# The last 96 rows of an MLP's output weights, moved to 24 lanes and to another DMA queue

## Chip, cores and metric

The kernel runs on one core of a Trainium2 chip. The metric is the device time of one execution in microseconds (us); the median of several timed runs counts, and lower is better. A profiled execution, taken separately, gives the trace. Engines: PE multiplies matrices, DVE (VectorE) works element by element, ACT (ScalarE) evaluates functions and copies, POOL (GpSimd) makes constants, SP (SyncE) only issues DMAs. ACT can issue DMAs too, in a queue of its own. A "lane" is one of the 128 partitions of the on-chip memory.

## What is computed

One decoding step of a transformer block: attention over a cache and a gated MLP, both on the same normalised input, added to that input. The input has 4 rows of 640 numbers; attention has 32 heads of 128 with a cache of 4096 positions; the MLP has 2 x 864 hidden units. All inputs are bf16.

```python
def _A_ref(x, k_cache, v_cache, wq, wo):
    q = (x @ wq).reshape(B, Sq, Hq, Dh).transpose(0, 2, 1, 3)
    scores = jnp.einsum('bhqd,bhkd->bhqk', q, k_cache) * Dh ** (-0.5)
    o = jnp.einsum('bhqk,bhkd->bhqd', _softmax(scores), v_cache)
    return o.transpose(0, 2, 1, 3).reshape(B, Sq, Hq * Dh) @ wo

def _B_ref(x, w_in, w_sp, b_sp, w_out):
    z = _gelu(jnp.einsum('bsd,df->bsf', x, w_in))
    z1, z2 = z[..., :Fh], _layernorm(z[..., Fh:])
    g = jnp.einsum('ts,bsf->btf', w_sp, z2) + b_sp[None, :, None]
    return jnp.einsum('bsf,fd->bsd', z1 * g, w_out)

xn = _layernorm(x)
return x + _A_ref(xn, ...) + _B_ref(xn, ...)
```

The two caches are 268 of the 282 MB that are read; everything else is small beside them.

## The kernel before

**Attention.** The work is cut into 16 units, one for each group of eight heads and batch row. A unit reads 8.4 MB of K and as much of V. Lane p holds 256 consecutive positions of one head. A unit's K comes in four runs of 64 positions a lane, into a ring of seven run buffers (`k_ring`); its V goes into one large buffer, `v_all`, of 64 KB a lane. For each run DVE multiplies K by the query (`product`, L493) and folds the halves (`fold_half`, L499), PE sums the folded products in eight steps (`sums`, L508), DVE finishes the row sums (`row_sums`, L521). Once a unit has its four runs come the maximum, the exponentials on ACT (L543), the spread by heads into `p_m` (L554) and the weighted sum over V on PE (`weighted`, L578), one unit later.

**Order.** The order on PE, DVE, ACT and SP is written by hand: the loop over n counts K runs, four for each unit. Loads stand in one list, `loads`, and are issued in that order on SP's queue by `pump()` as soon as the buffers they need are marked free. An issued load still waits, on SP, for the instructions that last used its buffer, and every load behind it on SP waits with it. DMA semaphores are dealt out in a circle of eight.

**The MLP.** Its weights have no buffer of their own. `w_q` and `w_in` lie in `v_all` before the first V load comes; the first 768 rows of `w_out` lie in `p_m` (six rows a lane, `w_out_sb`), and the last 96 rows, one a lane in lanes 0 to 95, lie in `v_all` behind `w_in` (`w_end_sb`, L101). `load_w` (L109 to L114) issues these three loads on SP between the two halves of the first unit's K. So SP's list begins: w_q, half of K of unit 0, w_in, w_out, the 96 rows, the other half of K of unit 0, K of unit 1, V of unit 0. V of unit 0 overwrites `w_in` and the 96 rows, and waits for the MLP's last products.

The generator `gmlp` (L351) does the MLP in pieces between the first K runs; `next(mlp)` runs it to its next `yield`. In order: the products with `w_in` (L361), 70 of them, with hidden units on the lanes of `zT`: for each half of the hidden units six groups of 128 lanes and, in the seventh column, one of 96; the copy to `zz` and GELU on DVE with a Tanh on ACT (L369 to L383); the sums for the layer norm (L388); its few scalars; the gate (L441 to L453); and the 14 products with `w_out` (L457), of which the last two use the 96 rows. They add into `out_ps`, where attention's projection (L639) adds later too. Piece one runs behind the sums of K run 0, two and three around the fold of run 1 and so on; the L457 products come after the fold of run 2 and before its sums, so on PE these sums stand behind them.

`NFC`, the number of groups of hidden units in each half (7), sets the width of all the tiles in between: `zz`, `gw`, `gt` have 2 x NFC x 4 = 56 columns, `gz` has three times 28, `yT` has 28.

Of the kernel before, what the change touches and what calls it, by code (L numbers as in the profile page):

```python
# [17 lines left out]
def kernel(  # L18
# [14 lines left out]
    nc = tc.nc  # L33
    P = nc.NUM_PARTITIONS
    Bsz, Sq, D = A_x.shape
    _, H, S, Dh = A_k_cache.shape
    HD = A_wq.shape[1]
    F = B_w_in.shape[1]
    Fh = F // 2
    DC = D // P  # L40
# [19 lines left out]
    QW = HC * Dh  # L60
    RING = 2 * NK - 1
    NFF = Fh // P
    NFC = NFF + 1
    FT = Fh - NFF * P
    NOH = D // 2
    CB = 4
    NG = NR // CB
# [25 lines left out]
    v_all = places.tile([P, NK * QW], BF16, name="v_all")  # L93
# [3 lines left out]
    w_in_sb = v_all[:, DC * HD : DC * (HD + F)].rearrange("p (c n) -> p c n", c=DC)  # L97
    w_out_sb = p_m[:].rearrange("p n g c h -> p (n g c h)")[:, 0 : NFF * D].rearrange(
        "p (k n) -> p k n", k=NFF
    )  # L100
    w_end_sb = v_all[:, DC * (HD + F) : DC * (HD + F) + D]  # L101
    nc.sync.dma_start(out=wq_sb, in_=A_wq.rearrange("(p c) n -> p c n", c=DC))

    wsp_bf = const.tile([1, 1], BF16)
# [4 lines left out]
    def load_w():  # L109
        nc.sync.dma_start(out=w_in_sb, in_=B_w_in.rearrange("(p c) n -> p c n", c=DC))  # L110
        nc.sync.dma_start(
            out=w_out_sb, in_=B_w_out[0 : NFF * P].rearrange("(p k) n -> p k n", k=NFF)
        )
        nc.sync.dma_start(out=w_end_sb[:FT], in_=B_w_out[NFF * P : Fh])  # L114

    def run_of(cache, u):
        hg, b = divmod(u, Bsz)
# [101 lines left out]
    for e in range(PAR):  # L219
        nc.gpsimd.tensor_copy(  # L220
            out=of_row[:, e, :, :, e, :],
            in_=ident[:].rearrange("p (k q) -> p q k", q=QD)[:, 0:Bsz, :, None].to_broadcast(
                [P, Bsz, NQ, LN]
            ),
# [15 lines left out]
    for i in range(NSTAT):  # L240
# [5 lines left out]
        out=rstd[:], in_=mv[:, 1:2], func=ACT.Sqrt, bias=eps_tile[:Bsz], scale=1.0  # L246
# [4 lines left out]
        out=xn_bf[:],  # L251
# [9 lines left out]
    for c in range(DC):  # L261
        nc.tensor.transpose(
            out=xnT_ps[:, c, :], in_=xn_v[:, c, :], identity=ident[:Bsz, :Bsz]
# [8 lines left out]
    for e in range(PAR):  # L272
        q_ps = ps_pv.tile([P, HG, Dh], FP32, tag="pv", name="q_ps")
        for c in range(DC):
            for k in range(NQ):
                nc.tensor.matmul(  # L276
                    out=q_ps[k * QD : (k + 1) * QD],
                    lhsT=xnT[:, c, :],
                    rhs=wq_v[:, c, k, e],
# [3 lines left out]
        rows = const.tile([P, HG, Dh], BF16, name=f"q_rows{e}")  # L283
        nc.vector.tensor_scalar(  # L284
            out=rows[:], in0=q_ps[:], scalar1=scale_qk, scalar2=None, op0=ALU.mult
# [7 lines left out]
        out=hot[:].rearrange("p c h -> p (c h)"),  # L293
        in_=ident[:].rearrange("p (g m) -> p m g", m=QD),
# [6 lines left out]
        out=pick[:, :, Bsz - 1 :].rearrange("p c (k q) -> p c k q", q=QD)[  # L301
            :, :, :, 0 : PAR * Bsz : Bsz
        ],
        in_=hot[:].rearrange("p c (e k) -> p c k e", e=PAR),
# [3 lines left out]
    with nc.allow_low_precision("0 and 1"):  # L308
        nc.vector.tensor_reduce(
            out=own[:],  # L310
            in_=ident[:].rearrange("p (h l) -> p h l", h=HT),
# [5 lines left out]
        out=par[:], in_=own[:].rearrange("p (k e) -> p e k", e=PAR), axis=AX.X, op=ALU.add  # L317
# [3 lines left out]
        out=far[:],  # L321
# [13 lines left out]
    for half in range(2):  # L335
        nc.tensor.matmul(
            out=out_ps[OG * half : OG * half + OG, :],
            lhsT=ident[:Bsz, :OG],
            rhs=x_bf[:, half * NOH : (half + 1) * NOH],
# [13 lines left out]
    def gmlp():  # L353
        zz, gw, gt, gz = (gm[n] for n in ("zz", "gw", "gt", "gz"))
        zT = ps_pv.tile([P, 2, NFC, Bsz], FP32, tag="pv", name="zT")
        for t in range(2):
            f1 = t * Fh + NFF * P
            w_t = w_in_sb[:, :, t * Fh : f1].rearrange("p c (f k) -> p c k f", k=NFF)
            for k in range(NFC):
                for c in range(DC):  # L360
                    nc.tensor.matmul(  # L361
                        out=zT[: P if k < NFF else FT, t, k, :],
                        lhsT=w_t[:, c, k, :] if k < NFF else w_in_sb[:, c, f1 : f1 + FT],
                        rhs=xnT[:, c, 0:Bsz],
                        start=(c == 0),
                        stop=(c == DC - 1),
                    )
        yield
        nc.vector.tensor_copy(out=zz[:, :, 0:NFF, :], in_=zT[:, :, 0:NFF, :])  # L369
        nc.vector.tensor_copy(out=zz[:FT, :, NFF, :], in_=zT[:FT, :, NFF, :])  # L370
        nc.vector.tensor_tensor(out=gw[:], in0=zz[:], in1=zz[:], op=ALU.mult)
        nc.vector.tensor_scalar(
            out=gw[:], in0=gw[:], scalar1=0.044715, scalar2=1.0, op0=ALU.mult, op1=ALU.add
        )
        nc.vector.tensor_tensor(out=gw[:], in0=gw[:], in1=zz[:], op=ALU.mult)
        nc.scalar.activation(
            out=gt[:], in_=gw[:], func=ACT.Tanh, scale=math.sqrt(2.0 / math.pi)
        )
        yield
        nc.vector.tensor_scalar(  # L380
            out=gt[:], in0=gt[:], scalar1=1.0, scalar2=0.5, op0=ALU.add, op1=ALU.mult
        )
        nc.vector.tensor_tensor(out=gz[:, 0:2], in0=zz[:], in1=gt[:], op=ALU.mult)  # L383
        sq = gz[:, 2, :, :]
        nc.vector.tensor_tensor(out=sq, in0=gz[:, 1, :, :], in1=gz[:, 1, :, :], op=ALU.mult)

        s_ps = ps_m.tile([1, 2, NFC, Bsz], FP32, tag="m", name="ln_ps")
        nc.tensor.matmul(  # L388
            out=s_ps[:], lhsT=ones_sq[:, 0:1], rhs=gz[:, 1:3], start=True, stop=True
        )  # L390
        yield
        st, ac = gm["st"], gm["ac"]
        mean_t = st[:, 0:Bsz]
        ex2_t = st[:, Bsz : 2 * Bsz]
        var_t = st[:, 2 * Bsz : 3 * Bsz]
        rst_t = st[:, 3 * Bsz : 4 * Bsz]
        tmp_t = st[:, 4 * Bsz : 5 * Bsz]
        nc.vector.tensor_reduce(
            out=st[:, 0 : 2 * Bsz].rearrange("o (s b) -> o s b", s=2),
            in_=s_ps[:].rearrange("o s k b -> o s b k"),  # L400
            axis=AX.X,
            op=ALU.add,
        )
        nc.vector.tensor_scalar(
            out=st[:, 0 : 2 * Bsz],
            in0=st[:, 0 : 2 * Bsz],
            scalar1=1.0 / float(Fh),
            scalar2=None,
            op0=ALU.mult,
        )  # L410
        nc.vector.tensor_tensor(out=tmp_t, in0=mean_t, in1=mean_t, op=ALU.mult)
        nc.vector.tensor_tensor(out=var_t, in0=ex2_t, in1=tmp_t, op=ALU.subtract)
        nc.scalar.activation(
            out=rst_t, in_=var_t, func=ACT.Sqrt, bias=eps_tile[:1], scale=1.0
        )
        wsp_t = work.tile([1, 1], FP32, name="wsp_t")
        nc.vector.tensor_copy(out=wsp_t[:], in_=wsp_bf[:])
        bsp_t = work.tile([1, 1], FP32, name="bsp_t")
        nc.vector.tensor_copy(out=bsp_t[:], in_=bsp_bf[:])
        yield  # L420
        nc.vector.reciprocal(out=rst_t, in_=rst_t)
        nc.vector.tensor_scalar(
            out=ac[:, 0:Bsz], in0=rst_t, scalar1=wsp_t[:, 0:1], scalar2=None, op0=ALU.mult
        )
        nc.vector.tensor_tensor(out=tmp_t, in0=ac[:, 0:Bsz], in1=mean_t, op=ALU.mult)
        nc.vector.tensor_scalar(
            out=ac[:, Bsz : 2 * Bsz],
            in0=tmp_t,
            scalar1=-1.0,
            scalar2=bsp_t[:, 0:1],  # L430
            op0=ALU.mult,
            op1=ALU.add,
        )
        ac_ps = ps_m.tile([P, 2 * Bsz], FP32, tag="m", name="ac_ps")
        nc.tensor.matmul(
            out=ac_ps[:], lhsT=ones_sq[0:1, :], rhs=ac[:], start=True, stop=True
        )
        ac_sb = work.tile([P, 2 * Bsz], FP32, name="ac_sb")
        nc.scalar.copy(out=ac_sb[:], in_=ac_ps[:])
        yield  # L440
        nc.vector.tensor_tensor(  # L441
            out=sq,
            in0=gz[:, 1, :, :],
            in1=ac_sb[:, None, 0:Bsz].to_broadcast([P, NFC, Bsz]),
            op=ALU.mult,
        )
        nc.vector.tensor_tensor(
            out=sq,
            in0=sq,
            in1=ac_sb[:, None, Bsz : 2 * Bsz].to_broadcast([P, NFC, Bsz]),  # L450
            op=ALU.add,
        )
        nc.vector.tensor_tensor(out=gm["yT"][:], in0=gz[:, 0, :, :], in1=sq, op=ALU.mult)  # L453
        for k in range(NFC):
            w = P if k < NFF else FT
            for half in range(2):
                nc.tensor.matmul(  # L457
                    out=out_sum(half),
                    lhsT=gm["yT"][:w, k, :],
                    rhs=(w_out_sb[:, k] if k < NFF else w_end_sb[:FT])[  # L460
                        :, half * NOH : (half + 1) * NOH
                    ],
                    start=False,
                    stop=False,
                )
        yield
# [206 lines left out]
    with tc.manual_schedule(engines={E.PE, E.DVE, E.Activation, E.SP}):  # L673
# [3 lines left out]
        for n in range(NK * NU):  # L677
# [55 lines left out]
            out=den[:],  # L733
# [62 lines left out]
```

## Time and profile before

| | us |
|---|---|
| timed runs, median of 3 (lowest to highest) | 662.78 (662.63 to 662.92) |
| the profiled execution | 667.55 |
| its span, from the first instruction to the last | 665.7 |
| DVE busy in the span | 522.6 (79%) |
| PE busy (matmul) | 307.7 (46%) |
| ACT busy | 29.7 (4%) |
| read from HBM | 282.24 MB, 424 GB/s over the span |

How to read it: "busy" is the time in which at least one instruction of the engine ran. The page cuts the span into 40 slices of 16.6 us and gives, for each, the busy share of every engine in tenths and what the core's 16 DMA engines moved. The table of queues gives packets, megabytes and the time their packets took, as a share of what 16 engines have. A packet is one contiguous piece that one DMA engine moves; a load of 128 lanes is 128 packets, eight for each engine, and at its end each engine adds one to the load's semaphore, by a packet of 4 bytes. The trace holds each packet with its start, duration and size, and each increment of a semaphore; where the text speaks of packet records or increments, it is these.

In lines of the timeline the first two numbers are the start and the duration in us, then come engine, line and operation, what is written and read, the shape, and how many such instructions are merged (x70); in brackets the engine's idle time before and what ended it. SPq and ACTq are the instructions that issue DMAs.

### The profile page before, as it was taken

What the parts mean: (1) busy time and instruction counts of PE and PEld (TensorE: products, weight loads), DVE (VectorE), ACT (ScalarE), POOL (GpSimd) and SP (SyncE); (2) the same over time, 40 slices, a digit from 0 to 9 for tenths busy, and PEclk for the clock granted to TensorE, in tenths of its full rate; (3) what the DMA queues carried; (4) which work ended last, traced back from release to release, by engine and by line L of the source; (5) the groups of instructions that cost most, each with busy time, mean ns of one, the idle gap of its engine ahead of it and who ended that gap; (6) DMA issues with size and microseconds to landing.
All of it is one profiled execution on the core that took longest, in us unless ns stands there. A gap on an engine that the chain in (4) does not pass through costs nothing.

```text
span 665.7 us, 4619 instructions
## 1 busy us (share of the span) xinstructions
PE 307.7 (46%) x1999; PEld 135.3 (20%) x1999; DVE 522.6 (79%) x326; ACT 29.7 (4%) x73; POOL 2.6 (0%) x12
## 2 busy tenths in 40 slices
PE   0264253624625364263536437263362634637357
PEld 0131021211302222122212212121120221213124
DVE  2576995969699594987959598595978969999950
ACT  0020000000000000000000000000000000000000
POOL 1000000000000000000000000000000000000000
PEclk9667586775767677586666867678585767866685
DMA  9999999999999999999999999999999999999996
GB/s 376 420 409 382 414 407 441 441 430 441 430 441 441 417 434 429 438 433 441 430 434 430 420 439 438 437 433 430 437 434 437 425 433 434 416 440 428 459 399 277
DMA packets 8417, 282.54 MB, mean 424 GB/s; under 512 B 865, under 2 KB 2125, under 8 KB 3277
## 3 DMA queue, kind: packets, MB, share of 16 engines
q1 hardware_dynamic: 8376, 282.24, 99.1%
q8 instruction: 15, 0.25, 0.1%
q14 instruction: 6, 0.04, 0.0%
q10 hardware_dynamic: 20, 0.01, 0.0%
HBM read 282.24 MB, written 0.01 MB: 424 GB/s over the span
## 4 chain that ended last, share of the span: by engine, by line
DMA 64%; DVE 26%; PE 8%; issue 1%; SPq 0%; DVEq 0%; ACT 0%
DMA k_ring<-in_A_k_cache_dram 57%; DVE k_ring L493 14%; DVE k_ring L499 7%; PE s_ps L508 7%; DMA v_all<-in_A_v_cache_dram 4%; DMA k_ring<-in_A_wo_dram 3%; DVE s_sb L521 2%; DVE p_m L554 1%; DVE m L530 1%; PE out_ps L639 1%; PE pv L578 1%; DVE mt L532 0%; DVE mt L535 0%; DVE nm L537 0%; DVE o_n L621 0%
## 5 line engine op out<-in xcount | busy, mean ns | idle before, releaser
L493 DVE TENSOR_TENSOR k_ring<-k_ring,qbc 128x8192 bf16<-128x8192 bf16 x64 | 282.7, 4418 | 96.8 <-DMA k_ring<-in_A_k_cache_dram 96.8
L508 PE MATMUL s_ps<-k_ring,ident 128*128 128x512 bf16 x512 | 197.8, 556 | 323.0 <-DVE k_ring L499 322.9
L508 PEld LDWEIGHTS <-ident 128*128 128x128 bf16 x512 | 64.7, 128 | 434.7 <-issue 381.5
L499 DVE TENSOR_TENSOR k_ring<-k_ring 128x4096 bf16<-128x4096 bf16 x64 | 146.0, 2281 | 0.0
L578 PE MATMUL pv<-v_all,p_m 128*32 128x512 bf16 x960 | 60.7, 410 | 0.0
L521 DVE TENSOR_REDUCE s_sb<-s_ps 128x64 f32<-128x512 f32 x64 | 43.7, 683 | 3.3 <-PE s_ps L508 3.3
L554 DVE TENSOR_TENSOR p_m<-p_c,own 128x2048 bf16<-128x2048 bf16 x16 | 36.6, 2285 | 0.7 <-ACT p_c L543 0.7
L578 PEld LDWEIGHTS <-p_m 128*32 128x32 bf16 x992 | 26.2, 104 | 41.5 <-issue 16.2
L543 ACT ACTIVATE p_c<-s_sb,nm 128x256 bf16<-128x256 f32 x16 | 8.1, 508 | 336.1 <-DVE nm L537 336.1
L609 PEld LDWEIGHTS o_ps<-o_rows,pick 128*128 128x128 f32 x96 | 20.7, 297 | 4.2 <-issue 3.2
L609 PE MATMUL o_ps<-o_rows,pick 128*128 128x128 f32 x96 | 19.6, 374 | 0.0
L590 ACT COPY o_rows<-pv 128x512 f32<-128x512 f32 x16 | 9.4, 585 | 168.8 <-PE pv L578 168.7
L284 DVE TENSOR_SCALAR q_rows<-q_ps 128x512 bf16<-128x512 f32 x2 | 1.4, 692 | 13.6 <-PE q_ps L276 13.6
L755 DVE TENSOR_TENSOR o_n_last<-o_last,rden_all 128x32 bf16<-128x32 f32 x1 | 0.2, 191 | 13.7 <-PE o_last L747 13.7
L483 ACT CAST qbc<-qbc_ps 128x128 bf16<-128x128 f32 x16 | 4.2, 265 | 105.2 <-PE qbc_ps L475 105.2
L276 PE MATMUL q_ps<-v_all,xnT 128*32 128x512 bf16 x40 | 3.8, 559 | 10.9 <-DMA v_all<-in_A_wq_dram 10.9
L530 DVE TENSOR_REDUCE m<-s_sb 128x1 f32<-128x256 f32 x16 | 6.7, 420 | 0.6
L475 PE MATMUL qbc_ps<-q_rows,of_row 128*128 128x128 bf16 x32 | 6.2, 284 | 0.6 <-DVE q_rows L284 0.6
L475 PEld LDWEIGHTS <-of_row 128*128 128x128 bf16 x32 | 4.3, 136 | 8.1 <-issue 7.6
L656 PE MATMUL o_last<-hot,o_rows 128*128 128x8 f32 x32 | 4.9, 279 | 0.7 <-ACT o_rows L590 0.7
L656 PEld LDWEIGHTS o_last<-hot,o_rows 128*128 128x128 f32 x32 | 4.8, 226 | 1.8 <-ACT o_rows L590 1.7
L578 PE MATMUL pv<-k_ring,p_m 128*32 128x512 bf16 x32 | 3.6, 631 | 2.8 <-DMA k_ring<-in_A_v_cache_dram 2.8
(88 smaller groups left out, 70.7 us busy)
## 6 DMA issues: line engine op xcount, KB each, us to landing
k_ring<-in_A_k_cache_dram SPq DMA_DIRECT2D x6, 4096.0 KB, 19.1
v_all<-in_A_v_cache_dram SPq DMA_DIRECT2D x2, 4096.0 KB
v_all<-in_A_wq_dram SPq DMA_DIRECT2D x1, 5120.0 KB
k_ring<-in_A_v_cache_dram SPq DMA_DIRECT2D x1, 4096.0 KB, 35.8
k_ring<-in_A_wo_dram SPq DMA_DIRECT2D x3, 1280.0 KB, 20.0
v_all<-in_B_w_in_dram SPq DMA_DIRECT2D x1, 2160.0 KB, 29.2
k_ring<-in_A_v_cache_dram SPq DMA_DIRECT2D x1, 2048.0 KB, 40.3
k_ring<-in_A_v_cache_dram SPq DMA_DIRECT2D x1, 1024.0 KB, 41.3
```

The lines of the kernel that those rows point to most:

```text
L475: nc.tensor.matmul(out=qb_ps[:], lhsT=of_row[:, e, b].rearrange("p k f l -> p (k f l)"), rhs=q_rows[e][:, hg, :], start=(e == 0), stop=(e ...
L493: nc.vector.tensor_tensor(out=t, in0=t, in1=qbcs[u][:, None, :].to_broadcast([P, HC, Dh]), op=ALU.mult)
L499: nc.vector.tensor_tensor(out=t[:, :, 0:HD2], in0=t[:, :, 0:HD2], in1=t[:, :, HD2:Dh], op=ALU.add)
L508: nc.tensor.matmul(out=s[:], lhsT=ident[:], rhs=t[:, :, g * RW : (g + 1) * RW], start=(g == 0), stop=(g == m - 1),)
L521: nc.vector.tensor_reduce(out=scores[u][:, r * HC : (r + 1) * HC], in_=sums_ps.pop(n)[:], axis=AX.X, op=ALU.add,)
L530: nc.vector.tensor_reduce(out=m1[:], in_=scores[u][:], axis=AX.X, op=ALU.max)
L543: nc.scalar.activation(out=p_c[u][:], in_=scores.pop(u)[:], func=ACT.Exp, bias=maxes.pop(u)[:], scale=1.0, accum_out=row_den[hg % NACC][:, ...
L554: nc.vector.tensor_tensor(out=p_m[:, u % 2], in0=p_c.pop(u)[:].rearrange("p (g c) -> p g c", c=CB)[:, :, :, None].to_broadcast([P, NG, CB, HT]
L578: nc.tensor.matmul(out=pvs[u][cg * QD : (cg + 1) * QD, :], lhsT=p_m[:, u % 2, g0 + n].rearrange("p c h -> p (c h)"), rhs=v_at[:, n * CB : ...
L590: nc.scalar.copy(out=o[:].rearrange("p c d -> p (c d)"), in_=pvs.pop(u)[:])
L609: nc.tensor.matmul(out=gr[hg][:], lhsT=pick[:, c, Bsz - 1 - b : P + Bsz - 1 - b], rhs=o[:, c, :], start=(b == 0 and c == 0), stop=(b == Bs ...
L656: nc.tensor.matmul(out=o_last[0][:, :, :, u % Bsz], lhsT=o[:, c, :], rhs=hot[:, c, :].rearrange("p (e k) -> p k e", e=PAR), start=(c == 0) ...
```

## The change

The 96 rows are laid out anew: row 4p + r of them goes to lane p, as the r-th of four in that lane, so they fill lanes 0 to 23 with 5,120 contiguous bytes each. The place in `v_all` is rounded up to a multiple of 256 elements. The load leaves SP's list; it is issued on ACT's queue instead, as four transfers, of which transfer l takes lanes l, l + 4, ..., l + 20. They stand in program order behind the products with `w_in` and so, on ACT, behind the second cast of a query (L483) and ahead of the table load for the Tanh (L376). The hidden units follow the rows: the last 96 of each half are taken in four groups of 24, every fourth unit, so NFC grows from 7 to 10, the products at L361 from 70 to 100 and those at L457 from 14 to 20, and the element-wise tiles from 56 to 80 and from 28 to 40 columns.

```diff
-    NFC = NFF + 1
-    FT = Fh - NFF * P
+    FR = 4
+    FT = (Fh - NFF * P) // FR
+    NFC = NFF + FR
+    LS = 4
...
-    w_end_sb = v_all[:, DC * (HD + F) : DC * (HD + F) + D]
+    end_at = -(-DC * (HD + F) // 256) * 256
+    w_end_sb = v_all[:, end_at : end_at + FR * D].rearrange("p (r n) -> p r n", r=FR)
...
-        nc.sync.dma_start(out=w_end_sb[:FT], in_=B_w_out[NFF * P : Fh])
+
+
+    def load_w_end():
+        rows = B_w_out[NFF * P : Fh].rearrange("(p r) n -> p r n", r=FR)
+        for l in range(LS):
+            nc.scalar.dma_start(out=w_end_sb[l:FT:LS], in_=rows[l:FT:LS])
...
-                        lhsT=w_t[:, c, k, :] if k < NFF else w_in_sb[:, c, f1 : f1 + FT],
+                        lhsT=w_t[:, c, k, :]
+                        if k < NFF
+                        else w_in_sb[:, c, f1 + k - NFF : f1 + FT * FR : FR],
...
+        load_w_end()
         yield
...
-        nc.vector.tensor_copy(out=zz[:FT, :, NFF, :], in_=zT[:FT, :, NFF, :])
+        nc.vector.tensor_copy(out=zz[:FT, :, NFF:], in_=zT[:FT, :, NFF:])
...
-                    rhs=(w_out_sb[:, k] if k < NFF else w_end_sb[:FT])[
+                    rhs=(w_out_sb[:, k] if k < NFF else w_end_sb[:FT, k - NFF])[
```

In the built program the order of the instructions on each engine is otherwise the same. On PE the first product with the 96 rows now waits for the four transfers' semaphores, where it waited for one. The semaphores of all later loads move three places round the circle.

## The prediction

> **What bounds the kernel now.** I read the page's slices first, then its DMA queues, then stretches of the span, and last the timeline around the edited transfer.
>
> ```profile
> DMA  9999999999999999999999999999999999999996
> GB/s 376 420 409 382 414 407 441 441 430 441 430 441 441 417 434 429 438 433 441 430 434 430 420 439 438 437 433 430 437 434 437 425 433 434 416 440 428 459 399 277
> ...
> q1 hardware_dynamic: 8376, 282.24, 99.1%
> q8 instruction: 15, 0.25, 0.1%
> ...
> q10 hardware_dynamic: 20, 0.01, 0.0%
> ```
>
> The 16 DMA engines are busy from the first slice to the last: no engine of the core sets the end, the queue of bytes does. q1 is SP's queue, q10 ScalarE's, q8 instruction fetches.
>
> ```profile
> 30.00:80.00 50.00, 21.29 (x132) 10.04 (x132) 40.37 (x41) 5.69 (x10) 0.00 (x0) 0.64 1.02 396
> 80.00:640.00 560.00, 264.64 (x1564) 113.09 (x1567) 468.34 (x260) 20.06 (x55) 0.00 (x0) 0.69 1.00 433
> ```
>
> Last column: GB/s. The queue runs at 433 for 560 us, but at 396 from 30 to 80 us, with the same DMA share: each packet is slower there (in the packet records a 64 KB packet takes 2.71 us instead of 2.42). That costs 50 x (1 - 396/433) = 4.3 us. The profiled execution took 667.55 us (span 665.7 and 1.9 around it), the runs 662.63 to 662.92: 4.8 us less, nearly this deficit. So I take the timed runs to be without it and put my sum on their median, 662.78. The terms are packet counts and durations, which hold in both.
>
> ```profile
> 36.26 3.37 PE L361 MATMUL zT<-xnT,v_all 128*128 128x4 bf16 x70
> 36.49 0.27 ACT L483 CAST qbc<-qbc_ps 128x128 bf16<-128x128 f32 x1 [15.17 <-PE qbc_ps L475]
> 36.77 1.28 ACT L376 ACT_TABLE_LOAD   x1
> ...
> 40.77 0.25 ACT L376 ACTIVATE gt<-gw 128x56 f32<-128x56 f32 x1 [2.71 <-DVE gw L375]
> ...
> 54.03 1.76 PE L457 MATMUL out_ps<-p_m,yT 128*4 128x320 bf16 x12 [2.68 <-DVE yT L453]
> 55.59 0.47 PE L457 MATMUL out_ps<-v_all,yT 96*4 96x320 bf16 x2
> ...
> 56.09 0.33 SPq L150 DMA_DIRECT2D v_all<-in_A_v_cache_dram  x1
> ...
> 66.91 4.42 DVE L493 TENSOR_TENSOR k_ring<-k_ring,qbc 128x8192 bf16<-128x8192 bf16 x1 [5.71 <-DMA k_ring<-in_A_k_cache_dram]
> ```
>
> The MLP's last two products (L457 on v_all) release the first V load (L150). It is issued 0.03 us after they end, and reaches the queue before the second K load (landed 66.9) is through. That lead is the only place where the MLP can touch the end.
>
> **The change part by part.** *Taken from SP's queue:* 96 rows of 1,280 B. In the packet records they are 6 packets of 55 ns per DMA engine: 6 x 0.055 = 0.33 us off each engine. SP's issue at 3.08 us (0.53) goes too; it is worth nothing, as SP then waits for a buffer until 36.28 (K load) with the queue full.
>
> *Put on ScalarE's queue:* four transfers of six rows of 5,120 B. q10's 20 packets tell how such transfers split: x_bf (4 rows) and one output (4 rows) are 4 data packets and 4 semaphore writes each, w_sp and b_sp (1 row) one and one: 8 + 8 + 2 + 2. So a six-row transfer is one data packet and one semaphore write on each of six engines. Packets of 5,120 B (w_o's loads) take 0.196, semaphore writes 0.009. w_sp's and b_sp's packets lie in one engine's sequence, so successive transfers begin at the same engine, and I put all four on the same six: 4 x 0.205 = 0.82 us on six engines, nothing on ten. Net: +0.49 on six engines, -0.33 on ten. If they spread instead, an engine gets at most two, 0.41, and the net is +0.08.
>
> Which engines decide? The 16 increments of the last w_o transfer's semaphore, one per engine, spread over 3.2 us: eight within 0.43 us of the last, eight at least 1.7 us earlier. The late eight got there by instruction fetches: the lag of one increment grows by some 1.5 us where a q8 packet falls. Six engines drawn blindly miss all eight in 28 of 8,008 cases, so the end most likely moves by +0.49; if the six are all early ones, by -0.33. I take **+0.5**.
>
> The Trainium skill's DMA: Bandwidth & Descriptors (Why a DMA increments its semaphore by 16 and not by 1) has a six-row HWDGE transfer run on the lowest-numbered six engines. By that the sum would also hold +0.49 on six engines, and the packet count of q10 agrees; no row tells which numbers the late engines have.
>
> *More work on PE and DVE:* the tail's products become four groups of 24 lanes. L361: 100 instead of 70 products, at 3.37/70 = 0.048 us: +1.44. L457: 20 instead of 14, the twelve starting 0.13 us apart: +0.78. DVE's element-wise tiles grow from 56 to 80 columns and from 28 to 40; L383 (56 columns, 216 ns) against L441 (28, 168) gives 1.7 ns a column, about 0.3 us for nine operations, the Tanh and the fp32 product. So the first V load is issued at 56.09 + 1.44 + 0.3 + 0.78 = 58.6.
>
> *What hides it.* In a run at 433 GB/s the queue starts the first unit's second half K load (4.19 MB) at 32.0 on its earliest engine and the second unit's load (8.39 MB) right behind, through at 32.0 + 12.58/0.433 = 61.1. An issue needs about 1.03 us to its first packet (w_q: issued 0.74, first packet 1.77). 58.6 + 1.03 = 59.6: 1.4 us of cover are left, 3.9 before. So this part costs 0, and one for one beyond 1.4. In the profiled execution, 4 us slower here, the cover is larger.
>
> *The new wait.* PE's 13th out_ps product now waits for four semaphores, at about 54.03 + 1.74 + 1.56 = 57.3. Behind it on PE stand its own eight products and the eighth-sums of the third K run (L508), which DVE's L521 waits for; the V load waits for PE. ScalarE issues after the cast at 36.49: from 36.8, each 0.23 to 0.57 (L106, L88), so 0.9 to 2.3 us; the table load ends by 40.4, the Tanh now comes at 42.3: hidden. No row shows a small transfer beside the K loads; the nearest is w_sp beside w_q: issued 1.33, data at 5.72, semaphore 7.24, b_sp's data 8.76, its semaphore 10.27, one SP packet of 1.51 between each. So the first data packet comes about 2.8 us after 36.8, at 39.6, and seven further turns follow, two behind 32 KB packets (1.21) and five behind 64 KB packets (2.42): 39.6 + 14.5 + 0.8 = 54.9, 1.5 more if an instruction fetch falls on the engine. Bounds: data and semaphore in one turn, 39.6 + 1.21 + 1.21 + 2.42 + 0.8 = 45; two SP packets a turn, 39.6 + 2.4 + 12 x 2.42 + 0.8 = 72. I take 55 to 56.5, by the nearest row: before 57.3, cost 0.
>
> The same page (Queues, rings and completion order) has an engine switch between queues only after a packet of about 9 to 17 descriptors. By that a turn could last nine 64 KB transfers, and the last semaphore would come far behind 72; the one-by-one order above speaks against it.
>
> *Moved without cost:* the tail's start in v_all (aligned to 256 elements), and the DMA semaphores, which shift three places round but are waited for at the same distance; the second K load then waits for a half load landed at 25.8.
>
> Sum: -0.33 + 0.82 = +0.49 on the deciding engines, everything else covered: 662.78 + 0.5 = **663.3 us**; for a profile like the one before, 665.7 + 0.5 = 666.2.
>
> **The rivals.**
> 1. *The six engines are not the late ones* (18%): -0.33, 662.45. For: fetches hit a fixed half of the engines. Against: the count above.
> 2. *The rows land late* (18%). From a landing past 57.3 the products wait, and from 58.7 the V load comes after the queue has run dry. One more 64 KB packet per transfer, 4 x 2.42 = 9.7, gives 56 + 9.7 = 65.7: 65.7 - 58.7 = 7 us on top of the forecast, 670.3; on two transfers only, 56 + 4.84 - 58.7 = 2.1, 665.4; the upper bound of 72 gives 13, 676.6. For: eight turns behind the largest packets and only 1.4 us of cover. Against: the one-to-one order beside w_q.
> 3. *A packet of another queue costs more than its own time* (12%). A 16 KB instruction fetch takes about 0.95 instead of the 0.61 of a 16 KB load, and the SP packet behind it 0.47 more: 2.3 times. At 2.3 the four data packets cost 1.84: +1.5, 664.3. Against: w_q's packets beside w_sp kept 1.51.
> 4. *The slow stage goes* (8%). It begins at 32 us, where the 96 short rows are, so they may start it. If the timed runs had it as well, its loss would give back 4.3: 658.5. Against: it ends at 78.6 on all engines at once, and the timed runs lie just where the queue would be without it.
>
> **How the numbers follow.** The forecast, +0.1 to +1.3, has 44%: 663.3. What a measurement tells from no change is about 0.2%, 1.3 us. Faster by more: rival 4, 8%. Slower by more: rivals 2 and 3, 30%. Within: forecast and rival 1, 62%. Range: down to 662.3, just under rival 1; up to 666, which holds rival 3 and the smaller delays of rival 2; outside stay 8% below and some 12% above.
>
> **What would show it.** q10 with 20 + 48 = 68 packets, q1 with 8,376 - 96 - 16 = 8,264; L361 x100 over 4.8 us; the V load at 58 to 59 directly behind L457; no slice under 9 in the DMA row. A V load later than 60, with DVE waiting for it or for K further on, is rival 2. GB/s of 430 and more from 30 to 80 would say only that the slow stage is no part of this kernel, unless the timed runs fall by 4 us too.

## The result, and the profile after

| | before | changed |
|---|---|---|
| timed runs, median of 6 each (lowest to highest), us | 662.77 (662.56 to 662.93) | 667.26 (667.08 to 668.11) |
| profiled execution, us | 667.55 | 667.36 |
| its span, us | 665.7 | 665.6 |

The ratio is 1.0069, 95% interval 1.0056 to 1.0082: 4.5 us slower, outside the predicted range. The two profiled executions are equally long, by accident: that of before held a slow stage (396 GB/s from 30 to 80 us) that its six timed runs and run e8 below do not have. The ratios below weigh single long executions in, which the medians do not: five of the 35 executions of the kernel before that e1 to e4 are compared with took 667.5 to 670.9 us, so the ratios of e1, e2 and e4 come out under 1 although their medians are the higher ones. The profile of the changed kernel says by itself where its time went. First the page, its slices and DMA queues:

```profile
DMA  9997999999999999999999999999999999999996
GB/s 376 438 448 325 435 429 421 418 441 441 430 441 438 414 437 438 429 437 438 438 434 434 429 422 434 441 442 429 433 426 441 434 431 431 415 430 439 448 408 264
...
q1 hardware_dynamic: 8264, 282.12, 98.4%
q8 instruction: 16, 0.26, 0.1%
q10 hardware_dynamic: 68, 0.13, 0.1%
```

The packets went where the change sends them: q1 lost 112 and q10 gained 48. But the fourth slice, 50 to 67 us, has a 7 in the DMA row and 325 GB/s. Stretches of the same trace narrow it down (last two columns: share of the DMA engines, GB/s):

```profile
55.00:60.00 5.00, 1.76 (x12) 0.62 (x12) 4.93 (x5) 0.00 (x0) 0.00 (x0) 0.50 0.98 426
60.00:65.00 5.00, 2.46 (x12) 0.85 (x13) 0.11 (x1) 0.00 (x0) 0.00 (x0) 0.50 0.50 163
65.00:70.00 5.00, 2.29 (x6) 0.69 (x5) 2.67 (x2) 0.00 (x0) 0.00 (x0) 0.71 0.67 275
...
80.00:640.00 560.00, 261.36 (x1571) 110.38 (x1573) 471.49 (x261) 20.32 (x56) 0.00 (x0) 0.70 1.00 433
```

Before 60 and from 80 on the queue is full at 426 and 433 GB/s; between 60 and 70 it is not. The timeline there and ahead of it:

```profile
36.22 4.22 PE L369 MATMUL zT<-xnT,v_all 128*128 128x4 bf16 x100
36.24 0.33 SPq L147 DMA_DIRECT2D k_ring<-in_A_k_cache_dram  x1
36.46 0.27 ACT L494 CAST qbc<-qbc_ps 128x128 bf16<-128x128 f32 x1 [14.73 <-PE qbc_ps L486]
40.48 2.95 ACTq L122 DMA_DIRECT2D v_all<-in_B_w_out_dram  x4
...
44.76 0.27 ACT L387 ACTIVATE gt<-gw 128x80 f32<-128x80 f32 x1
...
55.83 1.76 PE L468 MATMUL out_ps<-p_m,yT 128*4 128x320 bf16 x12 [2.72 <-DVE yT L464]
...
62.54 1.22 PE L468 MATMUL out_ps<-v_all,yT 24*4 24x320 bf16 x8 [4.94 <-DMA v_all<-in_B_w_out_dram]
...
63.80 0.33 SPq L158 DMA_DIRECT2D v_all<-in_A_v_cache_dram  x1
...
67.33 0.69 DVE L532 TENSOR_REDUCE s_sb<-s_ps 128x64 f32<-128x512 f32 x1 [7.21 <-PE s_ps L519]
```

(L369, L468, L158, L147, L504, L510, L519 and L532 were L361, L457, L150, L139, L493, L499, L508 and L521; in e9 and e10 they stand one line further still.) ScalarE's cast is over at 36.73, but its four transfers are issued from 40.48, 0.02 us after PE's semaphore counted the last of the 100 products, at 40.46. PE then stands 4.94 us before the products with the 96 rows. The V load comes at 63.80; in the packet records the last K packets end between 60.6 and 62.5 and the first of V begin between 64.8 and 65.5. That leaves each DMA engine idle for 3.5 us on average, and the first 16 packets of V take 3.19 us instead of 2.42: 3.5 + 0.8 = 4.3 us, nearly the 4.5 that the kernel lost.

The records of q10 show the rows on their way: data at 46.05, semaphore writes at 48.66, data at 51.08, and so on at 53.68, 56.10, 58.71 and 61.13, the last write at 61.88. These are the eight turns of the prediction: on each of the six engines data and semaphore writes alternate, with one 64 KB packet of SP's between each and the next. Only the last write had none ahead of it: SP's queue was dry by then, and the write came 0.2 us behind its data. The turns began 6.5 us later than the prediction said.

In the built program ScalarE's first transfer waits for the load of w_in and for PE's products with it. The rows lie in columns of `v_all` that `w_in` does not use, but in every fourth lane; with neighbouring lanes (e2) the wait is gone. So the program's waits seem to be put down as if the strided transfer touched all that lies between its lanes. This is the reading that the experiments had to test.

### The profile page after: what moved, and what is told of

Same layout as the page of the kernel before. It is cut to its first block, busy times and chain, and to the rows that moved or that the text cites. A ratio compares the mean times of both kernels' runs of the same rounds, so it can differ in the third digit from the quotient of the medians.

```text
span 665.6 us, 4696 instructions
## 1 busy us (share of the span) xinstructions
PE 306.0 (46%) x2035; PEld 132.6 (20%) x2035; DVE 522.8 (79%) x326; ACT 29.7 (4%) x73; POOL 2.7 (0%) x12
## 3 DMA queue, kind: packets, MB, share of 16 engines
q1 hardware_dynamic: 8264, 282.12, 98.4%
## 4 chain that ended last, share of the span: by engine, by line
DMA 67%; DVE 21%; PE 10%; issue 1%; ACTq 0%; SPq 0%; DVEq 0%; ACT 0%
DMA k_ring<-in_A_k_cache_dram 52%; DVE k_ring L504 11%; DMA v_all<-in_A_v_cache_dram 9%; PE s_ps L519 8%; DVE k_ring L510 6%; DMA k_ring<-in_A_wo_dram 3%; DMA v_all<-in_B_w_out_dram 3%; DVE s_sb L532 1%; PE pv L589 1%; DVE m L541 1%; PE zT L369 1%; PE out_ps L650 1%; DVE mt L543 0%; DVE mt L546 0%; DVE nm L548 0%
## 5 line engine op out<-in xcount | busy, mean ns | idle before, releaser
L504 DVE TENSOR_TENSOR k_ring<-k_ring,qbc 128x8192 bf16<-128x8192 bf16 x64 | 282.8, 4418 | 87.2 <-DMA k_ring<-in_A_k_cache_dram 87.2
L519 PE MATMUL s_ps<-k_ring,ident 128*128 128x512 bf16 x512 | 199.6, 560 | 317.9 <-DVE k_ring L510 317.9
L519 PEld LDWEIGHTS <-ident 128*128 128x128 bf16 x512 | 65.3, 129 | 431.2 <-issue 385.6
L510 DVE TENSOR_TENSOR k_ring<-k_ring 128x4096 bf16<-128x4096 bf16 x64 | 146.1, 2282 | 0.0
L589 PE MATMUL pv<-v_all,p_m 128*32 128x512 bf16 x960 | 58.7, 399 | 0.7 <-DMA v_all<-in_A_v_cache_dram 0.7
L532 DVE TENSOR_REDUCE s_sb<-s_ps 128x64 f32<-128x512 f32 x64 | 43.8, 684 | 10.9 <-PE s_ps L519 10.9
L620 PEld LDWEIGHTS o_ps<-o_rows,pick 128*128 128x128 f32 x96 | 18.2, 264 | 4.2 <-issue 3.3
L620 PE MATMUL o_ps<-o_rows,pick 128*128 128x128 f32 x96 | 17.2, 339 | 0.0
L758 PE MATMUL o_last<-p_m,k_ring 128*128 128x8 bf16 x128 | 4.0, 173 | 1.5 <-DMA k_ring<-in_A_v_cache_dram 1.5
L650 PE MATMUL out_ps<-k_ring,o_t 128*4 128x320 bf16 x48 | 4.4, 335 | 0.0
```

Source lines behind the costliest of these rows:

```text
L504: nc.vector.tensor_tensor(out=t, in0=t, in1=qbcs[u][:, None, :].to_broadcast([P, HC, Dh]), op=ALU.mult)
L510: nc.vector.tensor_tensor(out=t[:, :, 0:HD2], in0=t[:, :, 0:HD2], in1=t[:, :, HD2:Dh], op=ALU.add)
L519: nc.tensor.matmul(out=s[:], lhsT=ident[:], rhs=t[:, :, g * RW : (g + 1) * RW], start=(g == 0), stop=(g == m - 1),)
L532: nc.vector.tensor_reduce(out=scores[u][:, r * HC : (r + 1) * HC], in_=sums_ps.pop(n)[:], axis=AX.X, op=ALU.add,)
L589: nc.tensor.matmul(out=pvs[u][cg * QD : (cg + 1) * QD, :], lhsT=p_m[:, u % 2, g0 + n].rearrange("p c h -> p (c h)"), rhs=v_at[:, n * CB : ...
L620: nc.tensor.matmul(out=gr[hg][:], lhsT=pick[:, c, Bsz - 1 - b : P + Bsz - 1 - b], rhs=o[:, c, :], start=(b == 0 and c == 0), stop=(b == Bs ...
```

## The experiments

Diffs are against the changed kernel. Shared runs of the kernel before had medians of 662.75, 662.71 and 662.73 us.

**e1, one transfer of 24 neighbouring lanes.**

```diff
-        for l in range(LS):
-            nc.scalar.dma_start(out=w_end_sb[l:FT:LS], in_=rows[l:FT:LS])
+        nc.scalar.dma_start(out=w_end_sb[:FT], in_=rows)
```

> The four transfers of six lanes become one transfer of 24 lanes, in the same place on ScalarE's queue; all else as in the changed kernel. Theory A (the last semaphore comes too late, the first V load is issued at 63.8 and the DMA queue runs dry for some 4 us): one data packet or three and one semaphore per engine, so two to four turns between SP's packets instead of eight, landing by 50, first V load at 58 to 59, no dry stretch, 662.6 to 663.5. Theory B (the loss is the price of the rows on a second queue or of the four groups of 24 themselves: 72 more instructions on PE, a 16th instruction fetch, more columns on DVE): 666 to 667.5, as in the changed kernel.

Measured: 663.06 us, ratio 0.9991 (0.9969 to 1.0013). ScalarE issues at 36.52, the first data follows at 40.12, the last semaphore at 44.05, and the V load is issued at 58.13. q10 has 36 more packets, 24 of data and 12 semaphore writes: two lanes on each of 12 engines. The loss is gone; but wait, stride (the step of four lanes) and number of turns were taken away together.

**e2, four transfers of six neighbouring lanes.** Only the choice of lanes differs from the changed kernel.

```diff
-        for l in range(LS):
-            nc.scalar.dma_start(out=w_end_sb[l:FT:LS], in_=rows[l:FT:LS])
+        for l in range(0, FT, FT // LS):
+            nc.scalar.dma_start(out=w_end_sb[l : l + FT // LS], in_=rows[l : l + FT // LS])
```

> Four transfers of six lanes as in the changed kernel, but each of six neighbouring lanes instead of every fourth, and so without the wait for the products with w_in ahead of the first issue. Theory A, with the wait as its first half: ACT issues at 36.8 instead of 40.5, eight turns still, landing 57 to 59.5, first V load at 59 to 60.5, dry for at most 1 us: 662.9 to 664. If the wait did not matter and eight turns alone decide: landing at 61 and 666 to 667. Theory B: 667.

Measured: 663.59 us, ratio 0.999 (0.9963 to 1.0018). Its timeline:

```profile
36.64 1.32 ACTq L122 DMA_DIRECT2D v_all<-in_B_w_out_dram  x4
...
55.29 1.76 PE L468 MATMUL out_ps<-p_m,yT 128*4 128x320 bf16 x12 [2.72 <-DVE yT L464]
...
56.98 1.23 PE L468 MATMUL out_ps<-v_all,yT 24*4 24x320 bf16 x8
...
58.24 0.33 SPq L158 DMA_DIRECT2D v_all<-in_A_v_cache_dram  x1
```

Issue at 36.64, last semaphore at 55.62, no bracket on the last products: PE did not wait. Four transfers in turns do not hurt if they begin in time. (The first semaphore write and the second data packet came together here, near 41.7, so it was one turn less than eight.)

**e3, eight transfers of three lanes.**

```diff
-    LS = 4
+    LS = 8
```

> Eight transfers of three lanes instead of four of six: sixteen turns per engine, eight issues on ACT instead of four (some 2.8 us more). Theory A: the turns stop costing once SP's queue has run dry near 61, the rest lands at once, so the first V load comes at 64 to 66 and the time is 667 to 669.5. A rival in which each turn costs a whole SP packet whatever the queue holds: eight more turns of 2.4 us, 680 to 687. Theory B: within 1 us of the changed kernel.

Measured: 669.05 us, ratio 1.0084 (1.0059 to 1.011). It does not tell what it was made to tell. The timeline shows another road to the same end:

```profile
40.33 9.92 ACTq L122 DMA_DIRECT2D v_all<-in_B_w_out_dram  x8
...
51.57 0.27 ACT L387 ACTIVATE gt<-gw 128x80 f32<-128x80 f32 x1
...
62.64 1.76 PE L468 MATMUL out_ps<-p_m,yT 128*4 128x320 bf16 x12 [2.92 <-DMA v_all<-in_B_w_out_dram]
...
64.34 1.23 PE L468 MATMUL out_ps<-v_all,yT 24*4 24x320 bf16 x8
```

The eight issues hold ScalarE from 40.33 to 50.25, because the last, in the built program, waits for the first transfer's semaphore. The Tanh comes at 51.57 instead of 44.76, and even the first twelve products are late. A number in the expected range was reached partly by a delay that nobody had expected.

**e4, one transfer of 24 lanes on SP's queue,** in the place where the 96 rows had been loaded before; the regrouping of hidden units stays.

```diff
+        load_w_end()
...
-        for l in range(LS):
-            nc.scalar.dma_start(out=w_end_sb[l:FT:LS], in_=rows[l:FT:LS])
+        nc.sync.dma_start(out=w_end_sb[:FT], in_=rows)
...
-        load_w_end()
```

> The rows go as one transfer of 24 lanes on SP's queue, where the 96 rows went before; the four groups of 24, their 30 more products with w_in, 6 more with w_out and the wider tiles stay. Theory A: no turns at all, landing near 33, first V load at 58 to 59, 662.5 to 663.4. Theory B in the form that the groups and PE's longer program are what costs: 666 to 667.5; in the form that the second queue costs: 662.5 to 663.4.

Measured: 663.01 us, ratio 0.9986 (0.9962 to 1.0011), V load at 58.16. The 36 more products, the wider tiles and the 16th instruction fetch are covered: they delay the V load by 1.6 us against e8 and move the time by no more than can be resolved.

**e5, e6 and e7: the same rows issued later.** e5 and e6 put the transfer, or the four of e2, on ScalarE behind the Tanh; e7 puts the one transfer behind the copy of `ac_sb`.

```diff
-        load_w_end()
...
+        load_w_end()
```

> One transfer of 24 neighbouring lanes, issued on ACT behind the Tanh, near 42, later than the changed kernel's 40.5. Theory A1 (eight turns are what is too long, a late issue alone does no harm): first data near 46, two more turns behind 64 KB packets, landing 50 to 53, first V load at 58 to 58.5 as with the early single transfer, 662.8 to 663.4. Theory A2 (the late issue alone is enough, whatever the number of transfers): first V load past 61 and 665 to 667.

> Four transfers of six neighbouring lanes, issued on ACT behind the Tanh, near 42: the late issue and the eight turns of the changed kernel, without its step of four lanes and without its wait. Theory A (late issue and eight turns together): first data near 46, last semaphore at 61 to 63, first V load at 62.5 to 64.5, 666 to 668. If the step of four lanes was what cost: 663.3 to 663.9, as with the neighbouring lanes issued early.

> One transfer of 24 neighbouring lanes, issued on ACT only behind the copy of the gate's scalars, near 53. Few turns, nothing on ACT or DVE delayed by it: only the landing is late. Theory A: first data 56 to 59, two more turns, landing 61 to 63.5, first V load at 62.5 to 65, DMA share of 60 to 65 us well under 0.8, 665.5 to 668. Theory B (the loss comes from the number of small packets or from ACT's delay): 662.8 to 663.5.

Measured: e5 663.31 us, ratio 1.0017 (1.0003 to 1.0032); e6 668.45, ratio 1.009 (1.0073 to 1.0107); e7 668.58, ratio 1.0085 (1.007 to 1.01). The timeline of e6:

```profile
41.76 1.31 ACTq L122 DMA_DIRECT2D v_all<-in_B_w_out_dram  x4
...
55.20 1.76 PE L468 MATMUL out_ps<-p_m,yT 128*4 128x320 bf16 x12 [2.92 <-DVE yT L464]
...
63.54 1.23 PE L468 MATMUL out_ps<-v_all,yT 24*4 24x320 bf16 x8 [6.58 <-DMA v_all<-in_B_w_out_dram]
...
64.80 0.33 SPq L158 DMA_DIRECT2D v_all<-in_A_v_cache_dram  x1
```

Lanes side by side, quickly issued, and slow all the same, for they were issued at 41.76. e5, issued at 41.47, needs three turns (data at 45.6 and 48.5, semaphores at 51.4) and is through in time. e7 has the same three turns (55.8, 58.6, 61.5), begun too late. So neither the late issue nor the number of turns decides alone: their sum does, by whether the rows land before PE needs them.

**e8, the kernel before, profiled again.** No change against it.

> The kernel before once more, for its trace. If the slow stage (396 GB/s from 30 to 80 us) belongs to this kernel: again near 396 there and a profiled time near 667.5. If it was an accident of that one execution: 430 to 436 in that stretch, and a profiled time of 662.5 to 663.2, span near 661.

Measured: 663.01 us in one execution, span 661.2. The stretch that was slow in the first profile, and the V load:

```profile
30.00:80.00 50.00, 22.82 (x132) 10.62 (x132) 43.52 (x43) 5.69 (x10) 0.00 (x0) 0.64 1.02 437
...
56.61 0.33 SPq L150 DMA_DIRECT2D v_all<-in_A_v_cache_dram  x1
```

437 GB/s where the first profile had 396. The slow stage is not in every execution of this kernel; what starts it is not known.

**e9, the changed kernel without the wait.** The rows get 5 KB a lane of their own; two tiles that are first used after the MLP share this place. Transfers, lanes and order stay.

```diff
-    w_end_sb = v_all[:, end_at : end_at + FR * D].rearrange("p (r n) -> p r n", r=FR)
+    w_own = const.tile([P, FR * D], BF16, name="w_own")
+    w_end_sb = w_own[:].rearrange("p (r n) -> p r n", r=FR)
...
-        p_c[u] = small.tile([P, NR], BF16, name="p_c")
+        c0 = 4 * GW + u % 2 * NR
+        p_c[u] = w_own[:, c0 : c0 + NR]
...
-        o = taken[u] = small.tile([P, CB, Dh], FP32, name="o_rows")
+        o0 = u % 2 * 2 * GW
+        o = taken[u] = w_own[:, o0 : o0 + 2 * GW].bitcast(FP32).rearrange(
+            "p (c d) -> p c d", c=CB
+        )
```

> The changed kernel with its four strided transfers, but the 96 rows lie in a place of their own (5 KB a lane, later used for two other tiles) instead of beside w_in in v_all. In the built program ScalarE's first transfer then waits neither for w_in nor for the products with it. Theory A (that wait made the rows late): ScalarE issues from 36.5 to 37.0, first data by 42.4 at the latest (36.8 + the 5.6 us of the changed kernel), last semaphore at 55 to 59 after eight turns. Theory B (transfers of every fourth lane are slow by themselves): the first issue still ends only at 40 to 41 although nothing is waited for, and the last semaphore comes at 61 to 62. In both the first V load no longer depends on these rows, so it is issued at about 41, the DMA queue does not run dry and the time is 662.8 to 663.8; the issue and packet times tell A from B, not the total.

Measured: 662.74 us, ratio 1.0 (0.9991 to 1.001). Its timeline:

```profile
35.93 4.22 PE L370 MATMUL zT<-xnT,v_all 128*128 128x4 bf16 x100
...
36.18 2.95 ACTq L123 DMA_DIRECT2D w_own<-in_B_w_out_dram  x4
...
40.19 0.33 SPq L159 DMA_DIRECT2D v_all<-in_A_v_cache_dram  x1
...
56.90 1.23 PE L469 MATMUL out_ps<-w_own,yT 24*4 24x320 bf16 x8 [0.31 <-DMA w_own<-in_B_w_out_dram]
```

The strided transfers now start beside the products instead of behind them, at 36.18; first data at 40.15, last semaphore at 56.42, as theory A has it. (Five of the six engines were through at 54.65, the sixth was a turn behind.) Theory B is out: the issues are as long as in the changed kernel (2.95 us for four), but that alone delays nothing that matters.

**e10, late rows in a place of their own.** e6 with the place of e9: PE must wait, the V load need not.

> Four transfers of six neighbouring lanes, issued behind the Tanh as in the earlier run that took 668.45, but with the rows in the same place of their own, which the first V load does not overwrite. The rows should land at 62 to 63 again and PE should wait for them for some 6 us. Theory A (the loss goes only through the first V load, which came after the DMA queue had run dry): V load at about 41, no DMA slice under 9, 662.8 to 663.8. Theory B (PE's late products delay the sums behind them, and with these DVE and the ring of K, enough to cost time without the V load): 665 to 668.5, with the same V load at 41.

Measured: 667.72 us, ratio 1.0075 (1.0059 to 1.0092). Theory A, which was mine, fell. The timeline of e10:

```profile
40.34 0.33 SPq L159 DMA_DIRECT2D v_all<-in_A_v_cache_dram  x1
...
63.81 1.22 PE L469 MATMUL out_ps<-w_own,yT 24*4 24x320 bf16 x8 [7.07 <-DMA w_own<-in_B_w_out_dram]
...
68.60 0.69 DVE L533 TENSOR_REDUCE s_sb<-s_ps 128x64 f32<-128x512 f32 x1 [9.34 <-PE s_ps L520]
...
83.43 0.33 SPq L148 DMA_DIRECT2D k_ring<-in_A_k_cache_dram  x1
```

And stretches of e10 (last two columns: share of the DMA engines, GB/s):

```profile
60.00:65.00 5.00, 1.19 (x9) 0.40 (x10) 0.00 (x0) 0.00 (x0) 0.00 (x0) 0.50 0.99 412
80.00:85.00 5.00, 3.61 (x10) 1.31 (x9) 5.00 (x2) 0.27 (x1) 0.00 (x0) 0.50 0.63 215
```

The timeline of e9 has the last two of these steps, the row sums and the third K load, here:

```profile
61.69 0.69 DVE L533 TENSOR_REDUCE s_sb<-s_ps 128x64 f32<-128x512 f32 x1 [2.58 <-PE s_ps L520]
...
76.51 0.33 SPq L148 DMA_DIRECT2D k_ring<-in_A_k_cache_dram  x1
```

The V load is early and the queue is full at 60 to 65. It runs dry 20 us later: PE's sums stand behind the late products, DVE waits 9.34 us for them instead of 2.58, and the load of the third unit's K, which needs a run buffer back, is issued at 83.43 instead of 76.51, both 6.9 us later. Around that issue each DMA engine idles for 3.1 us on average. With 0.67 us on the first K packet of each this makes 3.8 of the 5.0 lost. Before the gap, SP's packets beside the rows were slower than in e9, by 0.7 us on each engine in sum (see the last section); the remaining 0.5 has not been placed.

All of it side by side, from the traces (the last column is the median; e8 is one execution, and e7's traced execution took 667.40):

| run | rows through | V load issued | third K load issued | us |
|---|---|---|---|---|
| e8 (kernel before) | | 56.61 | 75.72 | 663.01 |
| e4 (on SP's queue) | 33.3 | 58.16 | 76.32 | 663.01 |
| e1 | 44.1 | 58.13 | 76.36 | 663.06 |
| e5 | 52.4 | 57.87 | 76.22 | 663.31 |
| e2 | 55.6 | 58.24 | 76.19 | 663.59 |
| e9 | 56.4 | 40.19 | 76.51 | 662.74 |
| changed kernel | 61.9 | 63.80 | 81.94 | 667.26 |
| e7 | 62.1 | 63.87 | 81.93 | 668.58 |
| e10 | 62.5 | 40.34 | 83.43 | 667.72 |
| e3 | 62.7 | 65.60 | 83.96 | 669.05 |
| e6 | 62.8 | 64.80 | 83.14 | 668.45 |

No line has its rows through after 57 and a time under 667, and none the other way round. The packet records say that the loss arises at one place: the changed kernel has moved its first 24 MB as early as e9, to 0.1 us, is 4.3 us behind it at 26 MB, and stays 4.2 to 5.0 behind to the end. e10 is 0.5 us behind e9 at 33 MB and 4.8 at 36 MB. No version beat the kernel before.

## Why the prediction was wrong

*Taken from SP's queue, put on ScalarE's queue.* Counts and sizes were right: 8,264 and 68 packets, six engines a transfer, 196 ns of data and 9 ns of semaphore write. What it makes of the time, +0.5, stays open: e9 carries the same packets and stands at 662.74, within an interval of about 0.6 us to either side; e2 carries them too and stands at 663.59. Which engines end late was not tested.

*More work on PE and DVE.* Covered, as said, and smaller: 100 products took 4.22 us, not 4.8, and the V load of e4 and e2 came 1.6 us behind that of e8 (58.16 and 58.24 against 56.61), where the sum has 2.5. It came near the predicted 58.6 all the same, because the profile the sum started from had it 0.5 us earlier than e8.

*What hides it.* The threshold fits what was measured. By the sum the V load could be issued up to about 60.0 (58.6 and 1.4 of cover); it came at 63.80, 3.8 us too late, and the slower first packets add 0.8: 4.6 against 4.5 measured. The runs only enclose it: up to 58.24 (e2) the queue did not run dry, from 63.80 on it did, and no run has this load in between. But the sentence that this lead "is the only place where the MLP can touch the end" is wrong. The third K load is a second place, through PE's order, DVE's row sums and the ring. In the changed kernel that load is late too (81.94 against 76.51 in e9), but no second gap stands in its packet records, since the V load had been held back by nearly as much; e10 shows this path alone.

*The new wait.* This is the step that failed, in its term "ScalarE issues after the cast at 36.49: from 36.8". I looked at what the transfers stand behind on ScalarE and at who waits for them, not at what they themselves wait for. The first one waits for the products and is issued at 40.48, 3.7 us late.

A second term of the same sum was too small: from the issue to the first data 5.57 us pass, not 2.8. No working stands beside the 2.8, and w_sp, the row it leans on, took 4.39 (1.33 to 5.72). The four issues are long (0.68 to 0.79 us each), and SP's packets on the way are larger than beside w_q (64 KB, not 40); which of the two counts for how much, no run separates. (e9, with the same long issues from 36.18, took 3.97; e6, with short ones from 41.76, 4.44.)

So the first data came at 46.05 instead of 39.6. The seven turns behind it took 15.8 us where 15.3 were said, and that is luck: the sum has two behind 32 KB packets and five behind 64 KB, the trace six behind 64 KB and the last behind none. 61.9 instead of 54.9 is past PE's need of the rows at 57.6. By these figures, as an estimate, the wait alone would have put the rows at 54.9 + 3.7 = 58.6 and the V load 1.9 later, at 60.5, just past the cover; it took both terms to lose 4.5 us.

The Tanh was held up further than the sum has it, to 44.76 instead of 42.3, but PE's first twelve products came only 0.5 us later than in e2 (55.83 against 55.29).

e9 takes the wait away and keeps the long issues: 56.42, inside the predicted 55 to 56.5, at no cost (there the V load depends on the rows no longer, but PE waited only 0.31 us for them). That it fell inside is again partly luck: the first data came 0.5 us later than predicted, and five engines needed one turn less.

*The slow stage.* Leaving its 4.3 us out of the sum was right: e8 runs at 437 GB/s there, and by their length the six timed runs did not have it either, so rival 4 did not come true. Rival 3 is out for the changed kernel: SP's packets beside those of q10 kept their 2.42 us. With neighbouring lanes they did not (last section). Rival 1 can't be told from the forecast.

So rival 2, "the rows land late", came true, with a time inside the prices worked out for it (665.4 to 676.6), but for another reason: not more packets to a turn, which held at one, but a late start. That the time fell between those prices is therefore no support for their working.

## What to carry to other kernels

Before a transfer is moved, read in the built program what the transfer itself waits for: a destination of every n-th lane can take on waits for data that merely lies between. Small transfers beside a queue that is kept full should be counted in turns, data packets per engine and one more for the semaphore, each as long as the neighbour's packet; one transfer spread over many engines needs fewer turns than several on the same few. And where late data holds an engine, take everything behind it in that engine's order into the account: freeing the nearest waiter (e10) only brought out the next. The choice of lanes cuts both ways: neighbouring lanes spared the wait and the long issue, but slowed the other queue's packets beside them, and the step of four lanes did not.

## What the runs showed of the hardware

A semaphore write of 4 bytes takes a turn like a packet of 5,120 bytes: beside SP's 64 KB packets each came 2.4 to 2.6 us after the one before. The Trainium skill's DMA: Bandwidth & Descriptors (Queues, rings and completion order) has an engine switch queues only after a whole packet, there a group of typically about 9 to 17 descriptors. In the changed kernel the switch came after every single 64 KB packet of SP's (each one contiguous piece) from 46.05 to 61.13, and the measurement decides. From the first issue to the first data it took 3.6 us (e1, e2) to 5.6 and 5.8 us (changed kernel, e3) beside the full queue.

ScalarE's issue of six lanes took 0.68 to 0.79 us with every fourth lane, and 1.31 to 1.32 us for four such transfers with neighbouring lanes; a single transfer of 24 neighbouring lanes took 0.30. The stride costs this by itself, since e9, which waits for nothing, shows the same 2.95 us for four.

After the queue had run dry, the first 64 KB packet on each engine took 2.62 to 3.44 us (mean 3.19) instead of 2.42, the second again 2.42: running dry costs more than the gap.

Neighbouring lanes slow the packets beside them. SP's 64 KB packets in flight together with a data packet of q10 took 2.42 us with every fourth lane (means of 2.418 in the changed kernel, 2.425 in e3, 2.419 in e9), but 2.55 us with the same four transfers of neighbouring lanes (e2), 2.49 and 2.51 in e6 and e10, and 2.56 to 2.77 with one transfer of 24 neighbouring lanes (e1, e5, e7). It falls on nearly all of the 16 packets in flight at a time, though q10's rows lie on 6 or 12 engines. In sum an engine lost 0.4 to 0.7 us by it, against 0.03 in the changed kernel and e9. That fits the medians of e1, e2 and e5, 0.3 to 0.8 us above those of the kernel before, and e9's, which is not above; that it is their cause was not tested, nor why neighbouring lanes do it.
